# The last FFN step taken whole and put one place earlier, and a normalisation that also adds zero: attention and FFN in one kernel on Trainium2

## The chip, the cores and the metric

The kernel runs on one core of a Trainium2 chip. The metric is the device time of one execution in microseconds. The core's engines are named as in the profile: PE (matrix products), PEld (its weight loads), DVE (vector), ACT (activation functions and copies), POOL (GpSimd) and SP (which issues the transfers).

## The reference, cut to what matters

Attention over a window of 96 positions and 8 global keys, for 4 batches of 8 heads with 768 positions of 64 values; then an FFN over 3072 tokens of 512 values, with 2048 hidden values and a rational function between its two products.

```python
scores = 0.125 * q @ k.T - slope[h] * dist;  scores = where(keep, scores, -1e9)
p = exp(scores - max);  p = p / (sum(p) + 1e-9);  x = p @ v       # tokens x 512
h = x @ w_in                                                     # 3072 x 2048
P = a0 + a1*h + a2*h**2 + a3*h**3
Q = 1 + |b0|*|h| + |b1|*h**2
out = (P / (Q + 1e-6)) @ w_out                                   # 3072 x 512
```

## The kernel before, in words

**Tiling.** 12 chunks of 256 tokens are worked through. A chunk has 8 attention units (128 tokens, two heads) and 8 FFN steps (256 of the 2048 hidden values), so there are 96 of either, numbered on through the chunks. A large loop over t writes the code: in turn t it emits the parts of attention unit t, t-2, t-4, and those of FFN step f = t - 12. So the FFN runs twelve turns behind the attention, and the last turns hold FFN work alone.

**An attention unit** u transposes q and k on PE (tile `tk`), copies them on ACT, forms the scores `s` on PE, masks them on DVE into `pr`, takes the exponential on ACT (`st_soft`, L464), sums on DVE (`stats`), and normalises `pr` in `st_norm` (L476): two multiplications by 1/sum, of 128x256 values each (128x128 where a batch begins). The first 14 units do that on DVE, all later ones on POOL. Then `pr` is copied by a transfer (`raw`), transposed on PE (`tp`), copied (`pT`) and multiplied with v (`o`). From o come the FFN's inputs `xh` and `xl`, a high and a low part of x: ACT casts xh (L540), and DVE subtracts to get xl (L541).

**An FFN step** f has these parts:
- `st_ffn1` (L250): h, 128 x 2 x 256, one bank of PSUM; each half (y = 0, 1) takes 12 products of 256 columns (four pieces of x, three products of high and low parts each). There are two h tiles.
- `st_ew1`: ACT makes u, a and s from h (L274, L275, L276); `st_ew2`: DVE makes u from u and h (L281, L282), and `side(f)` adds a and s (L283); `st_ew3`: ACT takes Ln and Exp (L290, L291) to get 1/Q into the one tile r (written q in the rows).
- `st_ew4`: DVE corrects r and forms the quotient (L295, L296, L297), ACT casts its high part into g (L305), and `side(f)` subtracts for the low part of g (L306). side is POOL for every step but the last.
- `st_ffn2` (L326): 6 products of 512 columns for each half of the 256 tokens, summed in `acc` over the 8 steps of a chunk. With a chunk's last step, acc is copied to o (L332 for the last chunk) and sent out (L335).

A chunk's weights come as 32-bit halves of doubles: transfers bring `r` (L173), ACT or POOL scale (L180, L178), POOL and DVE join the pieces (L181, L182, L184), and later L201 and L202 split them into high and low parts. That goes on until about turn 30.

**Order.** A planner sets the order of the instructions of each engine by the priorities in the tables `PRI` and `PRI_A` and by its own estimate of when each is ready. From turn 36 on (`FIXED`) PE alone runs in the order in which the code is written.

**The last step** (f = 95). Its two halves are taken one after the other: first product of half 0, then that half's whole chain `last_half` (ew1 to ew4), then the first product of half 1, and its chain. All of it is written behind the second product of step 92, with the second products of steps 93, 94 and 95 behind it.

Of the kernel before, what the change touches and what calls it, by code (L numbers as in the profile page):

```python
# [14 lines left out]
ALU = mybir.AluOpType  # L15
# [32 lines left out]
           ffn1b=550, ew1=600, ew4=650, ew2=700, ffn2a=750, pT=800, ffn2b=850, dec=900, wsplit=990)  # L48
PRI_A = dict(PRI, ffn1a=800, pv=1650, qkE=950, x=1650, split=-700, ew3=2400, norm=1800, raw=1801, ffn1b=900, ew1=1050,
             ew4=850, ew2=2400, ffn2a=-400, pT=850, ffn2b=2050, dec=1850, wsplit=1090)  # L50
# [50 lines left out]
def tile_kernel(ctx: ExitStack, tc: tile.TileContext, q, k, v, n_global, n_local,  # L101
                w_in, w_out, ca, cb, out):
    nc = tc.nc
# [11 lines left out]
    NU = NCH * UPC  # L115
# [118 lines left out]
    def st_ffn1(f, y):  # L234
        c, j = divmod(f, FPC)
        if y == 0:
            hps[f] = pl.ps_h.tile(sh, F32, tag="h", name=f"h{f}")
        jw, fw = divmod((2 * j + y) * P, 2 * TOK)
        fs = slice(fw, fw + P)
        if c == 0 and not pl.split:  # L240
            for ct in range(NCT):
                nc.tensor.matmul(out=hps[f][:, y, :], lhsT=full[1, ct, jw][:, fs], rhs=xT[c][:, ct, :],  # L242
                                 start=(ct == 0), stop=(ct == NCT - 1))
            return
        xh, xl = xT[c]
        n = 0
        for ct in range(NCT):
            wh, wl = w_hi((1, ct, jw)), low[1, ct, jw]
            for w, x in ((wh, xh), (wh, xl), (wl, xh)):
                nc.tensor.matmul(out=hps[f][:, y, :], lhsT=w[:, fs], rhs=x[:, ct, :],  # L250
                                 start=(n == 0), stop=(n == 3 * NCT - 1))
                n += 1
# [5 lines left out]
    def is_last(f):  # L258
        return f == NU - 1 and not pl.split

    def side(f):
        return nc.vector if is_last(f) else nc.gpsimd

# [27 lines left out]
    def st_ew4(f, ys=BOTH):  # L293
        u, a, r = ew[f]["u"][:, ys], ew[f]["a"][:, ys], rps[f][:, ys]
        nc.vector.scalar_tensor_tensor(out=u, in0=u, scalar=a0, in1=r, op0=ALU.add, op1=ALU.mult)  # L295
        nc.vector.scalar_tensor_tensor(out=r, in0=a, scalar=q1, in1=r, op0=ALU.add, op1=ALU.mult)  # L296
        nc.vector.scalar_tensor_tensor(out=u, in0=r, scalar=2.0, in1=u, op0=ALU.subtract, op1=ALU.mult,  # L297
                                       reverse0=True)
        if f < FPC and not pl.split:
            gs[f] = u  # L300
            return
        if f not in gs:
            gs[f] = pl.ffn.tile([P, 2, 2, TOK], FR, tag="g", name=f"g{f}", bufs=pl.gbufs)
        g = gs[f]
        nc.scalar.copy(out=g[:, 0, ys], in_=u)  # L305
        side(f).tensor_tensor(out=g[:, 1, ys], in0=u, in1=g[:, 0, ys], op=ALU.subtract)  # L306

    def last_half(f, y):
        for st in (st_ew1, st_ew2, st_ew3, st_ew4):
            st(f, slice(y, y + 1))  # L310

    def st_ffn2(f, t):
        c, j = divmod(f, FPC)
# [157 lines left out]
    def st_norm(u):  # L471
        i = unit(u)[4]
        pr, st = prob[u]
        for x in range(2):
            d = blocks_of(pr[:, x], i)
            (nc.vector if u < NORMS else nc.gpsimd).tensor_scalar(  # L476
                out=d, in0=d, scalar1=st[:, 6 + x:7 + x], scalar2=None, op0=ALU.mult)

# [66 lines left out]
    def windowed():  # L547
        st_load(0, True)
        nc.sync.dma_start(out=ni[:, 0:2], in_=n_local.bitcast(I32).partition_broadcast(P))
        nc.sync.dma_start(out=ni[:, 2:4], in_=n_global.bitcast(I32).partition_broadcast(P))  # L550
        make_identity(nc, ident)
        for x in range(2):
            nc.gpsimd.memset(qzero[(1 - x) * D:(2 - x) * D, :, x, :], 0.0)
        nc.vector.tensor_copy(out=nf, in_=ni)
        nl, ng = nf[:, 0:1], nf[:, 2:3]
        scr = tmp("scr").rearrange("p a (b w) -> p (a b) w", w=P)
        scr = [scr[:, x, :] for x in range(4)]
        window_masks(nc, scr, mask0, masks, nl, ng)
        st_load(2, True)
        load_v(0)  # L560
        load_v(2)
        nc.vector.tensor_copy(out=ident_r, in_=ident)
        load_coef()

        base = tc.cur_priority
        for t in range(NU + LAG + F2):
            f = t - LAG
            pri = PRI_A if f < FPC else PRI
            u0 = t - 3 - run_of(t - 4)
            if t == FIXED:  # L570
                ctx.enter_context(tc.manual_schedule(engines={mybir.EngineType.PE}))

            def on(name, fn, u, *args):
                if 0 <= u < NU:
                    tc.cur_priority = base + 1000 * t + pri[name]
                    fn(u, *args)

            if t % 2 == 0:
                on("load", st_load, t + 4)
            if t > FIXED:  # L580
                on("pT", st_pT, t - 4)
            if t >= FIXED:
                on("qkT", st_qkT, t)
            on("score", st_score, t - 2)
            on("soft", st_soft, t - 2)
            on("ffn1a", st_ffn1, f, 0)
            if t < FIXED:
                on("qkT", st_qkT, t)
                if u0 % run_of(t - 4) == 0:
                    on("pv", st_pv, u0)  # L590
                    on("x", st_x, u0)
            on("qkE", st_qkE, t)
            if t:
                on("split", st_split, t + 1)
            if not is_last(f - 1):
                on("ew3", st_ew3, f - 1)
            on("norm", st_norm, t - 2)
            on("raw", st_raw, t - 2)
            if is_last(f):
                st_ew4(f - 1)  # L600
                last_half(f, 0)
                st_ffn1(f, 1)
                last_half(f, 1)
            else:
                on("ffn1b", st_ffn1, f, 1)
                on("ew1", st_ew1, f)
                if not is_last(f - 1):
                    on("ew4", st_ew4, f - 1)
                on("ew2", st_ew2, f)
            if t >= FIXED and u0 % 4 == 0:  # L610
                on("pv", st_pv, u0)
                on("x", st_x, u0)
            on("ffn2a", st_ffn2, f - F2, 0)
            if t < FIXED:
                on("pT", st_pT, t - 3)
            on("ffn2b", st_ffn2, f - F2, 1)
            for n, (kind, j) in enumerate(WSCHED.get(t, ())):
                tc.cur_priority = base + 1000 * t + pri["dec"] + 50 * n
                (load_win if kind else load_wout)(j)
            for n, key in enumerate(list(full)[SPLITS.get(f - 1, 0):SPLITS.get(f, 0)]):  # L620
                tc.cur_priority = base + 1000 * t + pri["wsplit"] + 4 * n
                split_w(key)
        tc.cur_priority = base + 1000 * (NU + LAG + F2 + 4)
# [154 lines left out]
```

## Time and profile before

| | |
|---|---|
| runs shown | 766.95, 763.85 and 766.6 us; median 766.6 us |
| profiled execution | 764.81 us, with a span of 763.0 us from its first to its last instruction |
| PE busy | 724.8 us, 95% of the span |
| DVE, ACT, POOL busy | 81%, 77%, 62% |
| mean granted PE clock | 0.983 of full speed |

The span is what the rows of the trace cover; 1.81 us of the execution's own time lie outside it. PE's matmuls are pipelined, so that one row's end overlaps the next row's start: what one of them costs is read from start to start.

### The profile page before, as it was taken

The numbers are of one execution on the slowest core, as the hardware profiler recorded it, in microseconds if no ns is written. First come the engines' busy times: TensorE is split into PE (matmuls) and PEld (weight loads), VectorE is DVE, ScalarE is ACT, GpSimd is POOL, SyncE is SP. The second block draws the span as 40 slices with busy tenths as digits, with TensorE's granted clock in tenths as the row PEclk, the third lists the DMA queues.
The fourth block names the chain that finished last, engine by engine and source line by source line (L and its number), as shares of the span: only waits on it lengthen the run. The fifth ranks groups of instructions, "written<-read, shape, count | busy, mean of one in ns | idle before, by whom it ended". The sixth has DMA issues, their size and how long they took to land.

```text
span 763.0 us, 15903 instructions
## 1 busy us (share of the span) xinstructions
PE 724.8 (95%) x4992; PEld 630.5 (83%) x4992; DVE 619.3 (81%) x1610; ACT 584.0 (77%) x1433; POOL 470.6 (62%) x502
## 2 busy tenths in 40 slices
PE   5579997999999999999999999999999999999985
PEld 4467665788999889989989889989989889988974
DVE  6989999887888888888788888888788888876663
ACT  6685867777978878877878878878888878875662
POOL 3575688979665666655656665665655765754440
PEclk9898998999999999999999999999999999999998
DMA  8665544232423433434433444434424333310000
GB/s 205 194 190 155 166 143 119 70 78 71 118 73 117 129 115 119 143 101 118 128 89 119 129 116 122 139 103 118 132 89 132 114 99 96 101 36 15 29 1 33
DMA packets 134014, 83.21 MB, mean 109 GB/s; under 512 B 85024, under 2 KB 114720, under 8 KB 133920
## 3 DMA queue, kind: packets, MB, share of 16 engines
q1 hardware_dynamic: 133920, 82.10, 36.9%
q8 instruction: 42, 0.69, 0.4%
q14 instruction: 52, 0.43, 0.2%
HBM read 35.92 MB, written 6.29 MB: 55 GB/s over the span
## 4 chain that ended last, share of the span: by engine, by line
PE 81%; DVE 7%; ACT 4%; DMA 4%; POOL 2%; issue 1%; SPq 0%; POOLq 0%; DVEq 0%; ACTq 0%
PE acc L326 32%; PE h L250 31%; PE o L518 5%; PE s L441 5%; PE tp L497 3%; DMA r<-in_moe_w_in_dram 2%; PE tk L380 2%; DVE r L182 1%; PE acc L321 1%; PE s L436 1%; PE h L242 1%; DMA r<-in_moe_w_out_dram 1%; DVE pr L454 1%; DMA raw<-pr 1%; DVE pr L476 1%
## 5 line engine op out<-in xcount | busy, mean ns | idle before, releaser
L326 PE MATMUL acc<-wout_h,g 128*128 128x512 f32 x704 | 238.5, 399 | 0.8 <-POOL g L306 0.8
L476 POOL TENSOR_SCALAR pr<-pr,stats 128x256 f32<-128x256 f32 (+1 forms) x164 | 143.7, 887 | 105.6 <-DVE stats L469 42.9
L250 PE MATMUL h<-xh,win_h 128*128 128x256 f32 x704 | 201.2, 286 | 4.8 <-DVE fu L282 4.8
L250 PE MATMUL h<-xl,win_h 128*128 128x256 f32 x704 | 199.5, 283 | 0.0
L283 POOL TENSOR_TENSOR fa<-fa,fs 128x512 f32<-128x512 f32 x95 | 125.2, 1318 | 83.3 <-ACT fs L276 80.3
L326 PEld LDWEIGHTS acc<-wout_h,g 128*128 128x128 f32 x704 | 131.6, 189 | 31.5 <-POOL g L306 2.5
L250 PEld LDWEIGHTS h<-xh,win_h 128*128 128x128 f32 x704 | 134.7, 191 | 7.1 <-DVE fu L282 5.5
L250 PEld LDWEIGHTS h<-xl,win_h 128*128 128x128 f32 x704 | 133.2, 189 | 2.1 <-issue 1.0
L306 POOL TENSOR_TENSOR g<-fu,g 128x512 fp32r<-128x512 f32 x87 | 113.4, 1303 | 22.9 <-ACT g L305 13.5
L295 DVE SCALAR_TENSOR_TENSOR fu<-fu,coef,q 128x512 f32<-128x512 f32 (+1 forms) x97 | 71.8, 740 | 40.7 <-ACT q L291 36.6
L464 ACT ACTIVATE pr<-pr,stats 128x256 f32<-128x256 f32 (+1 forms) x192 | 92.4, 483 | 14.0 <-DVE stats L454 12.8
L281 DVE TENSOR_TENSOR fu<-fu,h 128x512 f32<-128x512 f32 (+1 forms) x97 | 65.6, 676 | 39.4 <-ACT fs L276 39.3
L274 ACT ACTIVATE fu<-h,coef 128x512 f32<-128x512 f32 (+1 forms) x97 | 75.1, 774 | 25.8 <-PE h L250 21.2
L290 ACT ACTIVATE fs<-fa,coef 128x512 f32<-128x512 f32 (+1 forms) x97 | 69.6, 718 | 30.1 <-POOL fa L283 26.4
L416 ACT ACTIVATE qT<-tk 64x128 fp32r<-64x128 f32 x144 | 39.0, 271 | 50.8 <-PE s L441 42.3
L282 DVE SCALAR_TENSOR_TENSOR fu<-fu,coef,h 128x512 f32<-128x512 f32 (+1 forms) x97 | 71.4, 737 | 1.2
L296 DVE SCALAR_TENSOR_TENSOR q<-fa,coef,q 128x512 f32<-128x512 f32 (+1 forms) x97 | 72.1, 743 | 0.0
L297 DVE SCALAR_TENSOR_TENSOR fu<-q,fu 128x512 f32<-128x512 f32 (+1 forms) x97 | 66.2, 682 | 1.6
L275 ACT ACTIVATE fa<-h,coef 128x512 f32<-128x512 f32 (+1 forms) x97 | 65.5, 675 | 2.4 <-PE acc L321 2.4
L276 ACT ACTIVATE fs<-h,coef 128x512 f32<-128x512 f32 (+1 forms) x97 | 66.2, 683 | 0.0
L305 ACT CAST g<-fu 128x512 fp32r<-128x512 f32 (+1 forms) x89 | 55.3, 621 | 14.0 <-DVE fu L297 13.7
L454 DVE CUSTOM_DVE_ANT_0 pr<-s,masks 128x256 f32<-128x256 f32 x160 | 60.9, 416 | 2.0 <-PE s L436 0.8
(243 smaller groups left out, 1610.1 us busy)
## 6 DMA issues: line engine op xcount, KB each, us to landing
raw<-pr SPq DMA_DIRECT2D x58, 256.0 KB
sp<-nat SPq DMA_DIRECT2D x36, 256.0 KB
qT<-qT SPq DMA_DIRECT2D x144, 64.0 KB
r<-in_moe_w_in_dram SPq DMA_DIRECT2D x16, 512.0 KB
r<-in_moe_w_out_dram SPq DMA_DIRECT2D x16, 512.0 KB
nat<-in_q_dram SPq DMA_DIRECT2D x48, 128.0 KB
nat<-in_k_dram SPq DMA_DIRECT2D x48, 128.0 KB
vt<-in_v_dram SPq DMA_DIRECT2D x48, 128.0 KB
```

Source lines behind the costliest of these rows:

```text
L250: nc.tensor.matmul(out=hps[f][:, y, :], lhsT=w[:, fs], rhs=x[:, ct, :], start=(n == 0), stop=(n == 3 * NCT - 1))
L274: nc.scalar.activation(out=u, in_=h, func=AF.Identity, scale=a3, bias=a2)
L282: nc.vector.scalar_tensor_tensor(out=u, in0=u, scalar=a1, in1=h, op0=ALU.add, op1=ALU.mult)
L283: side(f).tensor_tensor(out=a, in0=a, in1=s, op=ALU.add)
L290: nc.scalar.activation(out=s, in_=a, func=AF.Ln, bias=q1)
L295: nc.vector.scalar_tensor_tensor(out=u, in0=u, scalar=a0, in1=r, op0=ALU.add, op1=ALU.mult)
L296: nc.vector.scalar_tensor_tensor(out=r, in0=a, scalar=q1, in1=r, op0=ALU.add, op1=ALU.mult)
L306: side(f).tensor_tensor(out=g[:, 1, ys], in0=u, in1=g[:, 0, ys], op=ALU.subtract)
L326: nc.tensor.matmul(out=acc, lhsT=gs[f][:, z, y, ts], rhs=w, start=(ft == 0 and n == 0), stop=(ft == NFT - 1 and n == 2))
L454: nc.vector.tensor_tensor_reduce(out=blocks_of(pr[:, x], i), in0=blocks_of(s_ps[:, x], i), in1=mk, scale=-(2.0 ** -(h + 1)), scalar=3e38, ...
L464: nc.scalar.activation(out=d, in_=d, func=AF.Exp, scale=-1.0, bias=st[:, x:x + 1], accum_out=st[:, 2 + 2 * x:3 + 2 * x])
L476: (nc.vector if u < NORMS else nc.gpsimd).tensor_scalar(out=d, in0=d, scalar1=st[:, 6 + x:7 + x], scalar2=None, op0=ALU.mult)
```

## The change

- P's normalisation (L476) gets a second operation, an addition of 0.0, on DVE and on POOL alike. Its result is the same.
- `last_half` goes. The last step has one chain over both halves, as every other step.
- PE's order at the end: both halves of the first product of step 95 stand right behind those of step 94, ahead of the second products of steps 92, 93 and 94.
- The addition of a and s (L283) and the subtraction for g (L306) of the last two steps, 94 and 95, are on DVE; before, those of step 95 alone.

```diff
     def side(f):
-        return nc.vector if is_last(f) else nc.gpsimd
+        return nc.vector if f >= NU - 2 and not pl.split else nc.gpsimd
...
-    def last_half(f, y):
-        for st in (st_ew1, st_ew2, st_ew3, st_ew4):
-            st(f, slice(y, y + 1))
...
             (nc.vector if u < NORMS else nc.gpsimd).tensor_scalar(
-                out=d, in0=d, scalar1=st[:, 6 + x:7 + x], scalar2=None, op0=ALU.mult)
+                out=d, in0=d, scalar1=st[:, 6 + x:7 + x], scalar2=0.0, op0=ALU.mult, op1=ALU.add)
...
-            on("ffn1a", st_ffn1, f, 0)
+            if not is_last(f):
+                on("ffn1a", st_ffn1, f, 0)
...
-            if not is_last(f - 1):
-                on("ew3", st_ew3, f - 1)
+            on("ew3", st_ew3, f - 1)
...
-            if is_last(f):
-                st_ew4(f - 1)
-                last_half(f, 0)
-                st_ffn1(f, 1)
-                last_half(f, 1)
-            else:
+            if not is_last(f):
                 on("ffn1b", st_ffn1, f, 1)
-                on("ew1", st_ew1, f)
-                if not is_last(f - 1):
-                    on("ew4", st_ew4, f - 1)
-                on("ew2", st_ew2, f)
+            if is_last(f + 1):
+                for y in range(2):
+                    on("ffn1b", st_ffn1, f + 1, y)
+            on("ew1", st_ew1, f)
+            on("ew4", st_ew4, f - 1)
+            on("ew2", st_ew2, f)
```

The rows below name an instruction by its line, operation and tiles (written<-read; a number behind a name is the step's or unit's, the one behind the underscore a buffer's). In the changed kernel the lines behind L306 stand four to seven lower, so that L541 becomes L537, L372 L368 and L332 L328.

**The end, on DVE.** Before, the work on the last step comes in halves (128x256), between the rows of step 94 (fu94, q94):

```order
L281 TENSOR_TENSOR fu95_9836<-fu95_9836,h95_9814 128x256
L283 TENSOR_TENSOR fa95_9837<-fa95_9837,fs95_9838 128x256
L297 SCALAR_TENSOR_TENSOR fu94_9787<-q94_9827,fu94_9787 128x512
L282 SCALAR_TENSOR_TENSOR fu95_9836<-fu95_9836,coef_64,h95_9814 128x256
L295 SCALAR_TENSOR_TENSOR fu95_9836<-fu95_9836,coef_64,q95_9845 128x256
L296 SCALAR_TENSOR_TENSOR q95_9845<-fa95_9837,coef_64,q95_9845 128x256
L297 SCALAR_TENSOR_TENSOR fu95_9836<-q95_9845,fu95_9836 128x256
L306 TENSOR_TENSOR g95_9851<-fu95_9836,g95_9851 128x256
L281 TENSOR_TENSOR fu95_9836<-fu95_9836,h95_9814 128x256
L283 TENSOR_TENSOR fa95_9837<-fa95_9837,fs95_9838 128x256
```

In the changed kernel, from the addition of a and s of step 94 on:

```order
L283 TENSOR_TENSOR fa94_9813<-fa94_9813,fs94_9814 128x512
L282 SCALAR_TENSOR_TENSOR fu94_9812<-fu94_9812,coef_64,h94_9759 128x512
L281 TENSOR_TENSOR fu95_9842<-fu95_9842,h95_9787 128x512
L283 TENSOR_TENSOR fa95_9843<-fa95_9843,fs95_9844 128x512
L295 SCALAR_TENSOR_TENSOR fu94_9812<-fu94_9812,coef_64,q94_9839 128x512
L296 SCALAR_TENSOR_TENSOR q94_9839<-fa94_9813,coef_64,q94_9839 128x512
L282 SCALAR_TENSOR_TENSOR fu95_9842<-fu95_9842,coef_64,h95_9787 128x512
L297 SCALAR_TENSOR_TENSOR fu94_9812<-q94_9839,fu94_9812 128x512
L306 TENSOR_TENSOR g94_9851<-fu94_9812,g94_9851 128x512
L295 SCALAR_TENSOR_TENSOR fu95_9842<-fu95_9842,coef_64,q95_9869 128x512
L296 SCALAR_TENSOR_TENSOR q95_9869<-fa95_9843,coef_64,q95_9869 128x512
L297 SCALAR_TENSOR_TENSOR fu95_9842<-q95_9869,fu95_9842 128x512
```

All rows are whole (128x512), and steps 94 and 95 alternate. L283 and L306 of step 94 are new on DVE; they came from POOL. L306 of step 95 and the copy of o follow.

**The end, on ACT.** Before, Ln of step 94 and then the halves of step 95:

```order
L290 ACTIVATE fs94_9789<-fa94_9788,coef_64 128x512
L274 ACTIVATE fu95_9836<-h95_9814,coef_64 128x256
L275 ACTIVATE fa95_9837<-h95_9814,coef_64 128x256
L291 ACTIVATE q94_9827<-fs94_9789 128x512
L276 ACTIVATE fs95_9838<-h95_9814,coef_64 128x256
L290 ACTIVATE fs95_9838<-fa95_9837,coef_64 128x256
L305 CAST g94_9833<-fu94_9787 128x512
L291 ACTIVATE q95_9845<-fs95_9838 128x256
L305 CAST g95_9851<-fu95_9836 128x256
L274 ACTIVATE fu95_9836<-h95_9814,coef_64 128x256
```

Now, from the first row of step 94 on:

```order
L274 ACTIVATE fu94_9812<-h94_9759,coef_64 128x512
L275 ACTIVATE fa94_9813<-h94_9759,coef_64 128x512
L276 ACTIVATE fs94_9814<-h94_9759,coef_64 128x512
L305 CAST g93_9821<-fu93_9732 128x512
L274 ACTIVATE fu95_9842<-h95_9787,coef_64 128x512
L275 ACTIVATE fa95_9843<-h95_9787,coef_64 128x512
L290 ACTIVATE fs94_9814<-fa94_9813,coef_64 128x512
L276 ACTIVATE fs95_9844<-h95_9787,coef_64 128x512
L291 ACTIVATE q94_9839<-fs94_9814 128x512
L290 ACTIVATE fs95_9844<-fa95_9843,coef_64 128x512
L305 CAST g94_9851<-fu94_9812 128x512
L291 ACTIVATE q95_9869<-fs95_9844 128x512
```

The three rows that read h95 stand ahead of Exp of step 94; Exp of step 95 stands behind the cast of g94.

**Turns 18 to 36, PE.** The planner's order changes here too, on all engines, though the text of the code does not. In turn 20, before (h8 is the first step of the second chunk, tk21 a transpose of q and k, tp17 and s19 attention):

```order
L250 MATMUL h8_1233<-xh1_705,w1_3_0l_1037 128x256
L497 MATMUL tp17_1283<-ident_70,pr17_1146 128x128 x4
L436 MATMUL s19_1319<-k2_203,qzero_69 128x256 x2
L372 MATMUL tk21_1343<-ident_70,nat20_909 128x128 x2
L518 MATMUL o8_1346<-pT17_1288,vt16_602 64x128 x2
```

Now:

```order
L368 MATMUL tk20_1246<-ident_70,nat20_909 128x128 x2
L250 MATMUL h8_1233<-xh1_705,win_h_59 128x256
L493 MATMUL tp17_1283<-ident_70,pr17_1146 128x128 x4
L432 MATMUL s19_1319<-k2_203,qzero_69 128x256 x2
L368 MATMUL tk21_1343<-ident_70,nat20_909 128x128 x2
L250 MATMUL h8_1233<-xl1_706,win_h_59 128x256
```

Seven of the 24 products of h8 now stand ahead of tp17, s19 and tk21, and 17 behind them; all 24 stood ahead.

**The same turns, DVE.** xl1 from o7 is an input of h8. Before:

```order
L281 TENSOR_TENSOR fu6_1088<-fu6_1088,h6_1068 128x512
L282 SCALAR_TENSOR_TENSOR fu6_1088<-fu6_1088,coef_64,h6_1068 128x512
L541 TENSOR_TENSOR xl1_706<-o7_1161,xh1_705 128x2x128
L182 SCALAR_TENSOR_TENSOR r0_13_1119<-r0_13_1119 128x512
L184 SCALAR_TENSOR_TENSOR w0_13f_1118<-w0_13f_1118,r0_13_1119 128x512
```

Now:

```order
L295 SCALAR_TENSOR_TENSOR fu6_1088<-fu6_1088,coef_64,q6_1176 128x512
L296 SCALAR_TENSOR_TENSOR q6_1176<-fa6_1089,coef_64,q6_1176 128x512
L184 SCALAR_TENSOR_TENSOR w0_15f_1132<-w0_15f_1132,r0_15_1133 128x512
L537 TENSOR_TENSOR xl1_706<-o7_1161,xh1_705 128x2x128
L281 TENSOR_TENSOR fu7_1185<-fu7_1185,h7_1153 128x512
```

xl1 from o7 stood ahead of the decoding of weights r0_13 to r0_15 (L182, L184); now it stands behind that of all three. On POOL the rows L181 of r0_13 and four of the splits L202 move ahead of one or two normalisations, and from turn 36 to the end the orders of DVE, ACT, POOL and SP differ in places by a row or two.

## Prediction

> **What bounds the kernel now.** I read the busy shares first, then the chain of waits, then the busy time by stretches of time.
>
> ```profile
> PE 724.8 (95%) x4992; PEld 630.5 (83%) x4992; DVE 619.3 (81%) x1610; ACT 584.0 (77%) x1433; POOL 470.6 (62%) x502
> PE 81%; DVE 7%; ACT 4%; DMA 4%; POOL 2%; issue 1%; SPq 0%; POOLq 0%; DVEq 0%; ACTq 0%
> ```
>
> PE is busy for 95% of the span, and 81% of the chain that ended last is PE's. In the stretches (columns: length, then each engine's busy time with its instructions, the granted PE clock, the transfers) the rest sits at the start and in two more places:
>
> ```profile
> 0.00:95.00 95.00, 74.11 (x354) 54.22 (x355) 81.57 (x238) 66.54 (x185) 54.08 (x67) 0.93 0.64 182
> 95.00:114.00 19.00, 17.77 (x86) 12.00 (x85) 19.00 (x38) 13.03 (x34) 15.50 (x16) 1.00 0.47 138
> 114.00:133.00 19.00, 15.13 (x81) 9.72 (x80) 17.27 (x29) 15.29 (x36) 16.44 (x18) 0.83 0.45 129
> 133.00:735.00 602.00, 601.16 (x4395) 540.65 (x4394) 489.55 (x1285) 478.96 (x1160) 380.63 (x401) 1.00 0.34 100
> 735.00:763.00 28.00, 16.62 (x82) 13.95 (x80) 11.89 (x23) 10.21 (x21) 3.92 (x4) 0.91 0.07 23
> ```
>
> From 133 us to 735 PE hardly idles: the row leaves it 0.8 us of 602. There a faster DVE, ACT or POOL has almost nothing to give. PE idles 20.9 us up to 95, where weights and the first units come in, in an order that the change keeps to turn 18, 1.23 us from 95 to 114 and 3.87 us from 114 to 133, where all engines are loaded, and at the end. The chain of waits at the end, in order of time (start, length, what):
>
> ```profile
> 733.27 2.83 PE h L250 x24
> 738.90 1.48 PE h L250 x12
> 744.53 0.40 DVE fu L282
> 744.97 2.93 PE h L250 x12
> 747.90 8.34 PE acc L326 x36
> ```
>
> The first half of h95 takes 1.48 us for 12 products. The second half starts at 744.97, when the first half's chain has left the bank: 4.59 us of idle PE. It then takes 2.93 us, because the clock has dropped:
>
> ```profile
> 744.00:745.00 1.00, 0.03 (x1) 0.03 (x1) 0.92 (x2) 0.94 (x2) 0.00 (x0) 0.70 0.00 0
> 745.00:746.00 1.00, 1.00 (x5) 1.00 (x6) 0.49 (x2) 0.47 (x2) 0.69 (x1) 0.50 0.00 0
> 748.00:749.00 1.00, 1.00 (x6) 0.83 (x5) 0.00 (x0) 1.00 (x3) 0.00 (x0) 1.00 0.00 0
> ```
>
> So the way of taking the last step costs 4.59 + 1.45 = 6.0 us of PE. Without it, PE would end near 750.2, if g95 were ready. It won't be; that sets the gain.
>
> **The change part by part: the end.** Durations of the rows I use (start, duration, engine):
>
> ```profile
> 736.13 0.78 ACT L274 ACTIVATE fu<-h,coef 128x512 f32<-128x512 f32 x1 [0.91 <-PE h L250]
> 736.82 0.68 ACT L275 ACTIVATE fa<-h,coef 128x512 f32<-128x512 f32 x1
> 737.38 0.69 ACT L276 ACTIVATE fs<-h,coef 128x512 f32<-128x512 f32 x1
> 737.96 0.62 ACT L305 CAST g<-fu 128x512 fp32r<-128x512 f32 x1
> 738.10 0.69 DVE L281 TENSOR_TENSOR fu<-fu,h 128x512 f32<-128x512 f32 x1 [0.71 <-ACT fs L276]
> 738.83 0.75 DVE L282 SCALAR_TENSOR_TENSOR fu<-fu,coef,h 128x512 f32<-128x512 f32 x1
> 739.41 1.28 POOL L306 TENSOR_TENSOR g<-fu,g 128x512 fp32r<-128x512 f32 x1
> 739.48 0.73 ACT L290 ACTIVATE fs<-fa,coef 128x512 f32<-128x512 f32 x1 [0.90 <-POOL fa L283]
> 741.22 0.60 ACT L291 ACTIVATE q<-fs 128x512 f32<-128x512 f32 x1
> 741.86 0.75 DVE L295 SCALAR_TENSOR_TENSOR fu<-fu,coef,q 128x512 f32<-128x512 f32 x1 [2.29 <-ACT q L291]
> 742.52 0.75 DVE L296 SCALAR_TENSOR_TENSOR q<-fa,coef,q 128x512 f32<-128x512 f32 x1
> 743.85 0.68 DVE L297 SCALAR_TENSOR_TENSOR fu<-q,fu 128x512 f32<-128x512 f32 x1
> ```
>
> From start to start an instruction that need not wait costs some 0.08 less than its duration on either engine (L295 to L296: 0.66; L274 to L275: 0.69). L281 starts when L276 ends, in this row; I keep that.
>
> I walk the new order from 736.10, where h94 ends (L274 reads it at 736.13), and leave all before it unmoved.
>
> 1. PE: h95 whole, 736.10 + 24 x 1.48/12 = 739.06 at most; at h94's pace of 2.83, 738.93. Its bank was read last by L282 of step 93, at 734. Then acc for 92 and 93, 2.8 each (36 products in 8.34): to 744.5. g93's subtraction is no longer behind L283 of step 94 on POOL and ends near 740, in time.
> 2. ACT: L274 and L275 of 95 at 738.96 and 739.65; Ln of 94 at 740.2; L276 of 95 at 740.9 to 741.55; Exp of 94 to 742.05. DVE: L281, L283, L282 of 94 from 738.10 to 740.1. L281 of 95 waits for L276: 741.6; L283 of 95 742.2; L295 of 94 742.8, L296 743.45, L282 of 95 744.1, L297 of 94 744.8 to 745.5.
> 3. ACT casts g94, 745.5 to 746.1. Exp of 95 is queued behind that cast: to 746.65. DVE subtracts for g94 (as L297, 0.69): to 746.85. Then L295, L296, L297 of 95: 746.8 to 748.9; cast to 749.55; subtraction to 750.3.
> 4. PE: acc of 94 can begin at 746.15, after 1.6 us of idling. Its third product needs the low part, 746.9, and ten more take 2.3: 749.2. acc of 95 begins at 749.6; its third product at 750.3; end 752.65. The copy of o and the way out stay as they are.
>
> PE ended at 756.24, so the end gains 3.6 us. The second products of steps 92 and 93 cover 5.6 us of the chain's wait, where before they covered none of it; what is late next is g94, then g95. If the clock fell in the gap of 1.6 us, up to 1.45 us would go (the row of 2.93 against 1.48). Above it fell between 744 and 745, over 3.6 us after PE fell idle, so I count nothing.
>
> One cost is left: L283 of 94 is now on DVE while POOL subtracts for g93, both with two inputs in SBUF. This pair of engines shows what that can cost:
>
> ```profile
> 126.09 0.68 DVE L184 SCALAR_TENSOR_TENSOR w_14f<-w_14f,r 128x512 int32<-128x512 int32 x1
> 126.69 1.75 DVE L184 SCALAR_TENSOR_TENSOR w_15f<-w_15f,r 128x512 int32<-128x512 int32 x1
> 126.09 1.80 POOL L283 TENSOR_TENSOR fa<-fa,fs 128x512 f32<-128x512 f32 x1
> ```
>
> Of two like instructions, the one that met POOL's L283 took 1.75 instead of 0.68. Here Ln of 94 has 0.8 us of slack behind L283, so that at most 0.3 to 0.5 us of a 1.07 us stall reaches the end. I take 0.2. Ends of this term: -4.2 and -1.5; taken: -3.4.
>
> The Trainium skill (SBUF — State Buffer, Who interferes with whom) speaks against moving L283: a DVE instruction with two SBUF inputs contends with a GpSimd instruction that reads SBUF. The rows of 1.75 and 1.80 agree. By that rule as an exclusive lock the whole 0.5 is paid, and the end gains 3.1 instead of 3.4.
>
> **The normalisation.** Rows of POOL by shape, with count, busy time and mean; and the range over all calls of two lines (min/median/max):
>
> ```profile
> L476 POOL TENSOR_SCALAR pr<-pr,stats 128x256 f32<-128x256 f32 x140 | 129.4, 935 | 95.1 <-DVE stats L469 42.2 <-ACT q L291 35.2 <-ACT fa L275 14.7
> L476 POOL TENSOR_SCALAR pr<-pr,stats 128x128 f32<-128x128 f32 x24 | 14.3, 609 | 10.5 <-ACT q L291 6.7 <-DMA raw<-pr 3.1 <-DVE stats L469 0.7
> L178 POOL TENSOR_SCALAR w_0f<-r 128x512 f32<-128x512 f32 x2 | 3.0, 1524 | 1.0 <-DMA r<-in_moe_w_in_dram 0.7 <-DVE stats L454 0.2
> L181 POOL TENSOR_SCALAR r<-r x32: 647/728/1510, 13.3 to 121.7; 128x512 int32<-128x512 uint16 x32
> ```
>
> L476 has one operation: 0.61 us for 128 columns and 0.93 for 256, so 2.5 ns a column and 0.28 fixed. L178, also one, fits: 1.52 for 512. L181 has two (multiply, add) and takes 0.65 for 512: 0.7 ns a column over the same 0.28. A second operation has thus no price here, and the nearest rows say that multiply-and-add runs three times faster than one multiplication. L181 reads 16-bit values and has constants for both operands, so it is near, not the same. Ends: 0.47 us (L181's pace) and 1.59 (twice L178's pace per column); I take 0.47 to 0.55, as L181 is the only row with two operations. POOL then loses some 65 us of its 470.
>
> What is it worth? From 133 us on at most those 0.8 us, most of them waits on other work: -0.2. On DVE the 28 early ones could gain or lose 0.1 each: nothing I can place, so 0.
>
> The Trainium skill (GPSIMD Engine Reference, 3.1 Elementwise) says that a body of up to two operations an element is bound by its ports at about one cycle, so that one and two cost alike. The rows of 1.52 and 0.65 differ from that. By it L476 would stay at 0.93, and the third rival below would hold.
>
> **The planner's new order, turns 18 to 36.** This edit costs most to price. The place before:
>
> ```profile
> 116.52 5.00 DMA r<-in_moe_w_out_dram
> 121.68 0.73 POOL L181 TENSOR_SCALAR r<-r 128x512 int32<-128x512 uint16 x1 [0.34 <-DMA r<-in_moe_w_out_dram]
> 122.49 2.37 DVE L182 SCALAR_TENSOR_TENSOR r<-r 128x512 int32<-128x512 int32 x2
> 119.75 0.42 DVE L541 TENSOR_TENSOR xl<-o,xh 128x256 fp32r<-128x256 f32 x1 [1.34 <-ACT xh L540]
> 126.74 0.69 PE L372 MATMUL tk<-ident,nat 128*128 128x128 f32 x2 [2.36 <-ACT k L402]
> 111.90 1.12 PE L321 MATMUL acc<-w_10f,fu 128*128 128x512 f32 x2 [1.04 <-DVE w_10f L184]
> ```
>
> xl1 from o7 (L541) was ready at 120.2, and h8 ran through. Now it stands on DVE behind the decoding of r0_15, whose transfer lands at 121.5 and whose L181 ends at 122.4. Behind it come L182 (0.7), the masks of unit 18 (0.75), a cast (0.5), L295 and L296 (1.3), L184 (0.7): xl1 near 126.9, some 6.7 us later. 17 products of h8 (2.0 us warm) then start behind it, and end near 129; o8, which stood at 128.5 before (tk21 waits 2.36 until 126.74, then PE waits again for pT), follows. Against that, w0_10 is decoded a place earlier, which takes most of the 1.04 us that PE waited at 111.90. Ends: -4 (both waits go, and the slow clock with them) and +4 (xl1 meets two stalls of 1.07 on DVE, and h8 runs at half clock, +2). I take +1.0: 0.5 to 1 later at o8, part of h8 slow, part of the 1.04 won. Behind 133 us PE is full, so this goes to the end as it is.
>
> On SP the transfers change places by a row or two, from turn 24 on; PE shows no wait for them after 133 us, so 0, with up to +0.5.
>
> **Sum.** -3.4 - 0.2 + 1.0 = -2.6 us on the execution of 764.81: 762.2. The median of the runs shown, 766.6, is 1.8 above that execution; in its terms I forecast 764.0, 0.3% faster. About 0.5% (3.8 us) is what a measurement can tell from no change.
>
> **The rivals.**
> - The planner's order gains. The PE waits at 111.90 (1.04) and ahead of tk21 (2.36) go, since POOL is done 0.4 us earlier with each normalisation and Ln follows it sooner. Then -3.4 - 0.2 - 2.6 = -6.2: 760.4. For it: ACT and DVE wait for POOL there. Against: xl1's new place, and r0_15, which no engine hastens.
> - Slower: xl1 comes still later. It decides if h8's rest starts past 131 us, 4 us behind my 126.9, with the clock at half: +7 there, net +3.4: 770.0. For it: POOL's splits collide with DVE there, and two or three stalls of 1.07 each would be needed. Against: ACT would still give PE its transposes.
> - The addition doesn't speed POOL up: L476 stays at 0.93 or grows. The end gains as computed, but the planner's order, if it reckons with a faster POOL, has L283 and the splits late: -3.4 + 2 = -1.4: 765.2.
> - The end gains less, as g94 or the clock is worse: -1.5 - 0.2 + 1.0: 765.9.
>
> **How the numbers follow.** Forecast 0.45; order gains 0.27; slower 0.08; no faster POOL 0.10; end gains less 0.10. Faster by over 0.5% (under 762.8): most of the order's case and a sixth of the forecast's, 0.33. Slower by over 0.5%: 0.05. The rest, 0.62, is within. The range leaves out the slower case and the far side of the order's gain: 759.8 to 767.8.
>
> **What would show it.** The end right: h95 as one run of 24 products right behind h94, PE's last row 3 to 4 us nearer to h94's end than the 20.1 us before, PE idle near 1.6 us ahead of acc of 94, clock 1.00. The norm right: L476 on POOL at 0.47 to 0.55. The order right: PE waits for xl1 (DVE L537) between 121 and 127 us. Wrong would be: PE idle above 1 us anywhere from 140 to 735, or a clock of 0.5 in the last 15 us.

## The result, and the profile after

| | before | after |
|---|---|---|
| median of 13 runs each | 766.95 us | 762.28 us |
| lowest and highest run | 763.85, 768.90 | 759.86, 765.46 |
| profiled execution (its span) | 764.81 (763.0) | 763.7 (761.9) |

The ratio is 0.9943, with a 95% interval of 0.9929 to 0.9957: 4.4 us faster, 3.3 to 5.4 us (the medians differ by 4.7). The forecast was 764.0 in a range of 759.8 to 767.8. The two profiled executions differ by only 1.1 us, since that of before lies 2.1 below its median and that of after 1.4 above its own. So the traces are compared part by part here, and the total is left to the medians.

PE's load, the stretches and the chain at the end of the changed kernel, as they were shown of before:

```profile
PE 728.0 (96%) x4992; PEld 633.4 (83%) x4992; DVE 621.1 (82%) x1605; ACT 580.6 (76%) x1427; POOL 397.8 (52%) x500
```

```profile
95.00:114.00 19.00, 18.19 (x86) 12.21 (x86) 19.00 (x37) 14.49 (x34) 12.86 (x15) 1.00 0.57 169
114.00:133.00 19.00, 13.33 (x53) 8.19 (x53) 16.02 (x31) 13.16 (x32) 16.70 (x18) 0.78 0.31 94
133.00:735.00 602.00, 602.00 (x4409) 542.37 (x4409) 491.58 (x1287) 477.93 (x1165) 315.92 (x402) 1.00 0.35 101
735.00:763.00 28.00, 18.65 (x100) 14.62 (x98) 13.40 (x20) 10.28 (x17) 4.39 (x3) 0.94 0.07 23
```

```profile
735.73 5.67 PE h L250 x48
741.48 0.41 ACT fu L274
742.16 0.68 ACT fa L275
742.84 0.61 ACT fs L290
747.32 0.61 DVE fu L297
747.96 0.63 ACT g L305
752.91 2.62 PE acc L322 x10
```

The row from 114 us shows PE worse off than before (13.33 against 15.13); from 133 us to 735 it now never idles (602.00). At the end the 4.59 us of idle PE and the half at slow clock are gone: h94 and h95 are one run of 48 products. What is left is a wait for g94 and a short one for g95 (timeline of PE; the bracket is the idle time ahead and what ended it):

```profile
748.63 0.50 PE L322 MATMUL acc<-wout_h,g 128*128 128x512 f32 x1 [1.64 <-ACT g L305]
752.11 0.50 PE L322 MATMUL acc<-wout_h,g 128*128 128x512 f32 x1 [0.15 <-ACT g L305]
```

And the normalisation on POOL, by shape, with its mean in ns:

```profile
L472 POOL TENSOR_SCALAR pr<-pr,stats 128x256 f32<-128x256 f32 x140 | 68.7, 504 | 93.4 <-DVE stats L465 64.8 <-ACT fa L275 10.9 <-DMA nat<-in_k_dram 9.8
```

It takes 504 ns instead of 935.

For the profiled executions I took three lengths from the timeline of PE: the start of h4 (the row `h<-x,w_2f` near 78 us, ahead of every row that the change moves), from there to the first product of h94, and from that to the end of PE's last row. The first row of before, and then all of after:

```profile
78.09 0.59 PE L242 MATMUL h<-x,w_2f 128*128 128x256 f32 x2
```

```profile
79.17 0.59 PE L242 MATMUL h<-x,w_2f 128*128 128x256 f32 x2
735.56 0.28 PE L250 MATMUL h<-xh,win_h 128*128 128x256 f32 x1
755.13 0.39 PE L322 MATMUL acc<-wout_h,g 128*128 128x512 f32 x1
```

So after: 79.17, then 735.56 - 79.17 = 656.39, then 755.13 + 0.39 - 735.56 = 19.96. The kernels named e1 to e11 are those of the next section. The last column is 45 us less PE's busy time in that stretch. One of the six executions of e10 took 1005.46 us at a mean granted clock of 0.658, and its ratio is that of the other five.

| kernel | start of h4 | to h94 | h94 to the end | PE idle, 95 to 140 us |
|---|---|---|---|---|
| before | 78.09 | 655.02 | 23.12 | 5.1 |
| after | 79.17 | 656.39 | 19.96 | 6.5 |
| e1 | 80.01 | 655.00 | 23.40 | 8.2 |
| e2 | 77.72 | 654.44 | 20.73 | 5.0 |
| e3 | 79.81 | 653.67 | 19.73 | 6.0 |
| e4 | 77.14 | 654.13 | 19.03 | 6.3 |
| e5 | 78.89 | 654.36 | 19.04 | 6.8 |
| e8 | 75.74 | 655.74 | 19.83 | 6.3 |
| e11 | 77.52 | 654.20 | 19.93 | 5.9 |

The first column scatters over 4.3 us among kernels whose rows up to there stand in the same order: one profile tells the start to no better than that. The clock that PE was granted up to 75 us goes with it in part: it was 0.93 in e8, which starts h4 first, and 0.86, 0.86 and 0.84 in the three that start it last (after, e3, e1), but 0.91 in e5, which is hardly earlier, and 0.86 in e2. The third column repeats to 0.3 us wherever the end is the same (before and e1; after and e11; e4 and e5), with one exception (e2, below). The kernels left out of the table have another order or pace on the way; their third column is 19.05 (e6), 19.91 (e7), 20.72 (e9) and 17.94 (e10).

### The profile page after: what moved, and what is told of

It is laid out like the page before. It is cut to its first block, busy times and chain, and to the rows that moved or that the text cites. A ratio compares the mean times of both kernels' runs of the same rounds, so it can differ in the third digit from the quotient of the medians.

```text
span 761.9 us, 15909 instructions
## 1 busy us (share of the span) xinstructions
PE 728.0 (96%) x4992; PEld 633.4 (83%) x4992; DVE 621.1 (82%) x1605; ACT 580.6 (76%) x1427; POOL 397.8 (52%) x500
## 4 chain that ended last, share of the span: by engine, by line
PE 83%; DVE 8%; issue 2%; POOL 2%; ACT 1%; DMA 1%; SPq 1%; ACTq 0%; DVEq 0%; POOLq 0%
PE h L250 33%; PE acc L322 32%; PE o L514 5%; PE s L437 5%; PE tp L493 4%; PE s L432 2%; DVE r L182 2%; PE tk L376 2%; PE acc L317 1%; DMA r<-in_moe_w_in_dram 1%; DVE pr L472 1%; DVE fu L295 1%; POOL r L181 1%; DVE pr L450 1%; DVE q L296 1%
## 5 line engine op out<-in xcount | busy, mean ns | idle before, releaser
L283 POOL TENSOR_TENSOR fa<-fa,fs 128x512 f32<-128x512 f32 x94 | 122.3, 1301 | 147.2 <-ACT fs L276 133.3
L472 POOL TENSOR_SCALAR pr<-pr,stats 128x256 f32<-128x256 f32 (+1 forms) x164 | 77.4, 485 | 114.4 <-DVE stats L465 70.3
L306 POOL TENSOR_TENSOR g<-fu,g 128x512 fp32r<-128x512 f32 x86 | 112.7, 1310 | 19.6 <-DVE qT L417 12.9
L281 DVE TENSOR_TENSOR fu<-fu,h 128x512 f32<-128x512 f32 x96 | 65.7, 684 | 45.1 <-ACT fs L276 45.0
L290 ACT ACTIVATE fs<-fa,coef 128x512 f32<-128x512 f32 x96 | 69.6, 725 | 35.4 <-POOL fa L283 33.4
L274 ACT ACTIVATE fu<-h,coef 128x512 f32<-128x512 f32 x96 | 74.7, 778 | 28.6 <-PE h L250 24.3
L295 DVE SCALAR_TENSOR_TENSOR fu<-fu,coef,q 128x512 f32<-128x512 f32 x96 | 71.5, 745 | 26.5 <-ACT q L291 24.1
L282 DVE SCALAR_TENSOR_TENSOR fu<-fu,coef,h 128x512 f32<-128x512 f32 x96 | 71.2, 741 | 1.0
L296 DVE SCALAR_TENSOR_TENSOR q<-fa,coef,q 128x512 f32<-128x512 f32 x96 | 71.8, 748 | 0.0
L297 DVE SCALAR_TENSOR_TENSOR fu<-q,fu 128x512 f32<-128x512 f32 x96 | 66.1, 688 | 1.2
L275 ACT ACTIVATE fa<-h,coef 128x512 f32<-128x512 f32 x96 | 65.2, 679 | 2.2 <-PE acc L317 2.2
L276 ACT ACTIVATE fs<-h,coef 128x512 f32<-128x512 f32 x96 | 66.0, 687 | 0.0
```

Of the source, the lines that this page charges most:

```text
L274: nc.scalar.activation(out=u, in_=h, func=AF.Identity, scale=a3, bias=a2)
L282: nc.vector.scalar_tensor_tensor(out=u, in0=u, scalar=a1, in1=h, op0=ALU.add, op1=ALU.mult)
L283: side(f).tensor_tensor(out=a, in0=a, in1=s, op=ALU.add)
L290: nc.scalar.activation(out=s, in_=a, func=AF.Ln, bias=q1)
L472: (nc.vector if u < NORMS else nc.gpsimd).tensor_scalar(out=d, in0=d, scalar1=st[:, 6 + x:7 + x], scalar2=0.0, op0=ALU.mult, op1=ALU.add)
```

## The experiments

Ratios are to the kernel before, run beside them on the same chip.

**e1, the zero alone.**

```diff
 the kernel before, and in st_norm:
-  scalar2=None, op0=ALU.mult)
+  scalar2=0.0, op0=ALU.mult, op1=ALU.add)
```

> The kernel before with the zero added in the normalisation and nothing else; its instruction order up to the last steps is that of the changed kernel. Theory A (the end gave 3.0 us of the 4.4, the zero the other 1.4 by a quicker start): 1.4 us faster than before, ratio 0.998, PE idle of 4 to 5 us ahead of the second half of h95 as before. Theory B (the end gave all, the two starts differ by chance): within 0.5 us, ratio 1.000. Theory C (the zero gave most): 3 us or more, ratio 0.996 or less. Under all of them POOL's normalisation of 128x256 takes 0.50 us instead of 0.93.

Measured: 0.9992 (0.9974 to 1.0011), 765.97 against 766.42 us. L476 on POOL is at 0.48 us (median of both shapes). Theory C falls; A and B both lie in the interval.

**e2, the end alone.**

```diff
 the changed kernel, and in st_norm:
-  scalar2=0.0, op0=ALU.mult, op1=ALU.add)
+  scalar2=None, op0=ALU.mult)
```

> The changed kernel with one multiplication in the normalisation, as before; up to the last steps its instructions stand as in the kernel before. Theory A: 3.0 us faster than before, ratio 0.996; from the start of h94 to PE's last row 20.0 us, as in the changed kernel (23.0 before). Theory B: 4.4 us, ratio 0.994. Theory C: 1.5 us or less, ratio 0.998. If the zero's faster POOL helped at the end too, the 20.0 us would be longer here.

Measured: 0.9966 (0.9946 to 0.9986), 2.6 us. The zero and the end add up: 0.6 + 2.6 = 3.2 us. A's 0.996 fits and B's 0.994 lies just outside; C's 0.998 is inside, but e1 showed that the zero is not the larger part. The end was 20.73 us long, 0.77 more than after, with the same idle time of 1.64 ahead of g94. The stretches around it (length, busy times, then PE's clock) show why:

```profile
743.00:744.00 1.00, 0.58 (x3) 0.14 (x1) 1.00 (x3) 0.00 (x0) 0.00 (x0) 1.00 0.00 0
744.00:745.00 1.00, 0.00 (x0) 0.00 (x0) 0.52 (x1) 0.45 (x1) 0.00 (x0) 1.00 0.00 0
746.00:747.00 1.00, 1.00 (x4) 0.83 (x5) 1.00 (x2) 0.00 (x0) 0.00 (x0) 0.85 0.00 0
747.00:748.00 1.00, 1.00 (x3) 0.78 (x3) 0.91 (x2) 0.00 (x0) 0.00 (x0) 0.50 0.00 0
```

PE stopped near 743.6. The clock fell to half at about 746.7 (0.85 is the mean of that microsecond), 3.1 us later and after PE was back at work, and stayed there to 750. In the six profiles with this idle time (after, e2, e7, e8, e9, e11) it fell in two: in e9 at about 771.5 us, 3.0 us after PE had stopped, and there too the end is some 0.8 us longer (20.72). And with the zero missing, three waits of PE are back, 0.8 us in sum. They stand in the waits of PE from 140 to 730 us, as in the kernel before, whose row is:

```profile
PE acc L326 <- POOL g L306: 0.8, 3, 0.3
```

In the changed kernel that list is empty.

**e3, h95 whole, but in its own turn.**

```diff
 the changed kernel, and in the loop:
-            if not is_last(f):
-                on("ffn1a", st_ffn1, f, 0)
+            on("ffn1a", st_ffn1, f, 0)
 ...
-            if not is_last(f):
-                on("ffn1b", st_ffn1, f, 1)
-            if is_last(f + 1):
-                for y in range(2):
-                    on("ffn1b", st_ffn1, f + 1, y)
+            on("ffn1b", st_ffn1, f, 1)
```

> The changed kernel with the first product of step 95 whole, but in its own turn, behind the second product of step 92. Theory A (h95 ahead of step 92 puts L274 and L275 of step 95 ahead of Ln of 94 on ACT, and this costs step 94 more than the earlier h95 wins): 0.6 us faster than the changed kernel, ratio to before 0.993 to 0.994; from h94's start to PE's last row 19.4 us. Rival (the early place of h95 is what makes the end short): 1.5 to 2.8 us slower than the changed kernel, 21.5 to 22.8 us, since h95 starts 2.8 us later.

Measured: 0.9942 (0.9922 to 0.9963); the end 19.73 us. The rival falls: the early place of h95 wins nothing. The end is shorter than the changed kernel's, as A says, but by 0.2 us and not 0.6: PE waits 0.69 for the low part of g94 and 1.08 for g95. What gained at the end was to take step 95 whole, not to take it early.

**e4, the last rows of ACT and DVE in written order.**

```diff
 the changed kernel, in the turn of step 95:
+            by_hand.enter_context(tc.manual_schedule(engines={PE, Activation, DVE}))
 st_ew3(94); st_ew1(95)
-            on("ew4", st_ew4, f - 1)
-            on("ew2", st_ew2, f)
+            st_ew4(f - 1, last=lambda: st_add(f))   # L283 of 95 ahead of L306 of 94
+            st_mul(f)                               # L281, L282 of 95
```

> The changed kernel with the last rows of ACT and DVE in an order written out: step 94's Ln and Exp ahead of step 95's L274, and 94's L295 to L297 ahead of 95's L281; all else in the same order. Theory A (the 1.64 us that PE waits for g94 come from that order): the wait ahead of the second product of 94 goes, PE's last row stands 18.3 us behind h94's start instead of 20.0, ratio to before about 0.992. Rival (the length of step 95's own chain sets the end whatever the order): 19.7 to 20.3 us, no difference to the changed kernel.

Measured: 0.9931 (0.9909 to 0.9953); the end 19.03 us, so that the rival falls. The wait for g94 went, as A says, but 0.7 of the 1.7 expected did not come: now PE waits 1.45 for g95, since DVE has no gap left. Exp of 95 (ACT L298) was done at 743.17; L302 of 95 started at 744.04, behind L289 and L290 of 95, which had been behind L315 of 94:

```profile
746.94 0.50 PE L331 MATMUL acc<-wout_h,g 128*128 128x512 f32 x1 [1.45 <-ACT g L312]
742.57 0.60 ACT L298 ACTIVATE q<-fs 128x512 f32<-128x512 f32 x1
743.19 0.75 DVE L290 SCALAR_TENSOR_TENSOR fu<-fu,coef,h 128x512 f32<-128x512 f32 x1
744.04 0.75 DVE L302 SCALAR_TENSOR_TENSOR fu<-fu,coef,q 128x512 f32<-128x512 f32 x1
```

**e5, the zero from unit 40 on, end as e4.**

```diff
 e4, and in st_norm:
+            if u >= 40: ... scalar2=0.0, op0=ALU.mult, op1=ALU.add
+            else:       ... scalar2=None, op0=ALU.mult
```

> The changed kernel with the last rows of ACT and DVE by hand, and the zero added only from unit 40 on: the early instructions stand as in the kernel before, POOL's normalisation is short from about 170 us on. Theory A (in the steady part the zero is worth 0.84 us, three waits of PE of 0.28 for POOL's g, and the new early order costs 1 to 2 us of PE): no wait of PE over 0.15 us from 140 us to the end part; PE idles 5.0 us from 95 to 140 us (6 to 8 with the zero everywhere); 1 us faster than with the zero everywhere, ratio to before 0.991 to 0.992. Theory B (the early order is worth nothing either way; starts differ by chance): same as with the zero everywhere, 0.993. Theory C (the early order gains): 0.994 or more.

Measured: 0.9918 (0.9888 to 0.9947), which tells A from B as little as from C. In its trace PE idled 6.8 us from 95 to 140, not 5.0, with the instructions as before; and one of the three waits of 0.28 stayed, at 263 us. Inconclusive on the early order.

**e7, the zero up to unit 39 alone.**

```diff
 the changed kernel, and in st_norm:
+            if u < 40: ... scalar2=0.0, op0=ALU.mult, op1=ALU.add
+            else:      ... scalar2=None, op0=ALU.mult
```

> The changed kernel with the zero added only up to unit 39. Theory A: PE's three waits of 0.28 us for POOL's g, near 260, 430 and 600 us, are back, since POOL's normalisation takes 0.93 us there; from 95 to 140 us PE idles as in the changed kernel, 6 to 8 us. Rival (those waits went with the new order, not with the short normalisation): they stay away.

One run: 776.64 us, 10 us slower than before, which neither theory had. Waits of PE from 140 to 730 us (sum, count, longest):

```profile
PE acc L322 <- ACT g L305: 4.0, 2, 2.0
PE acc L322 <- POOL g L306: 3.8, 4, 2.3
```

The rows of PE and of POOL there:

```profile
325.01 0.50 PE L322 MATMUL acc<-wout_h,g 128*128 128x512 f32 x1 [2.03 <-ACT g L305]
328.09 1.22 PE L322 MATMUL acc<-wout_h,g 128*128 128x512 f32 x2 [2.34 <-POOL g L306]
324.98 1.82 POOL L476 TENSOR_SCALAR pr<-pr,stats 128x256 f32<-128x256 f32 x2 [5.31 <-ACT g L305]
326.77 1.27 POOL L306 TENSOR_TENSOR g<-fu,g 128x512 fp32r<-128x512 f32 x1
```

PE's rows stand as in the changed kernel; those of DVE, ACT and POOL don't. At 323 us the cast of g is late, and on POOL two normalisations, 0.91 each, stand ahead of the subtraction for the same g, so that PE waits 2.03 and then 2.34 us; at 361 us it waits 2.01 and 0.87 in the same way. Two of the three 0.28s came back (447, 618 us), as A says. So at 0.93 us a normalisation, POOL's place in the steady part hangs on how the planner's order falls.

**e9, a maximum as the second operation.**

```diff
-  scalar2=0.0, op0=ALU.mult, op1=ALU.add)
+  scalar2=0.0, op0=ALU.mult, op1=ALU.max)
```

> The changed kernel with a maximum with 0.0 as the second operation in place of the addition (the values are positive, so nothing changes); the order of the instructions follows its own plan. Theory A (it is the pair of multiply and add that POOL runs quickly): L472 on POOL takes 0.93 us or more for 128x256, as with one multiplication. Rival (any second operation makes it quick): 0.50 us.

```profile
L472 POOL TENSOR_SCALAR pr<-pr,stats 128x256 f32<-128x256 f32 x140 | 160.4, 1157 | 65.4 <-DVE stats L465 49.5 <-ACT q L291 7.4 <-ACT fs L290 5.9
```

```profile
PE acc L322 <- POOL g L306: 7.5, 13, 2.0
PE acc L322 <- ACT g L305: 4.0, 2, 2.0
```

One run: 786.97 us. The instruction takes 1157 ns, more than the 935 of one multiplication: the rival falls. Not a second operation as such makes L472 short, but this pair. With 1.16 us a call PE waits 11.5 us for g between 140 and 730 us (the two rows of waits), with 0.93 it waits 0.8 us in the kernel before and 7.8 in e7, and with 0.50 in the changed kernel not at all. The planner's order differs in each, so this is the worth of the pace and of the order made for it.

**e8, only the last step's L283 and L306 on DVE.**

```diff
-        return nc.vector if f >= NU - 2 and not pl.split else nc.gpsimd
+        return nc.vector if is_last(f) else nc.gpsimd
```

> The changed kernel with L283 and L306 of step 94 on POOL, as before; those of 95 alone on DVE. Theory A (POOL would take 1.30 instead of 0.69 for each, but starts L283 of 94 at once, and DVE wins two places): Ln of 94 no later than 0.1 us, the low part of g94 0.6 later; from h94's start to PE's last row 19.6 to 20.6 us against 20.0. Rival (moving them to DVE was what made the end short): 21.2 us or more.

One run: 759.46 us; the end 19.83 us against 19.96. PE waits 0.67 us for the low part of g94, which now comes from POOL, but no longer for g95. Moving step 94's two instructions to DVE is worth nothing in this profile, as A says.

**e11, the zero on POOL alone.** The edit: DVE's normalisations have one multiplication.

> The changed kernel with the zero on POOL alone; the 28 normalisations on DVE have one multiplication, as before. The order of the instructions is that of the changed kernel. Theory A (on DVE the zero is worth nothing): ratio to before 0.994 to 0.995, as the changed kernel; L472 on DVE at 0.35 us, like with the zero. Rival (the later start of the kernels with the zero, 77 to 80 us against 78 at the first whole h, comes from a slower DVE): 1 us faster than the changed kernel, 0.993, and the 20 DVE rows of 128x256 shorter than with the zero.

Measured: 0.9946 (0.9925 to 0.9967). On DVE the 128x256 form takes 467 ns in the mean here and 517 in the changed kernel, but 435 and 468 in e3 and e4, which have the zero too: the zero isn't seen on DVE. The start of h4 at 77.52 lies within the scatter. The rival falls.

**e6, the zero in the scaling of the weights too, end as e4.**

```diff
 e4, and at L178:
-  scalar1=2.0 ** -112, scalar2=None, op0=ALU.mult)
+  scalar1=2.0 ** -112, scalar2=0.0, op0=ALU.mult, op1=ALU.add)
```

> The changed kernel with the last rows by hand, and with a zero added also in the scaling of the weights on POOL (L178, 12 calls of 1.5 to 2.1 us, 128x512). Theory A (multiply-and-add runs on POOL at the pace of L181, 0.7 ns a column): L178 takes 0.65 to 0.75 us, POOL wins 11 to 14 us ahead of 95 us; PE's idle time up to 60 us, 19.2 to 19.8 us, gets shorter by 0 to 2 us, the rest of it set by transfers and DVE; ratio to before 0.991 to 0.993. Rival (in that part transfers and DVE set everything, and a new order there costs): L178 short all the same, ratio 0.993 to 0.996.

Measured: 0.9886 (0.9861 to 0.9910), 757.65 us: the gain is more than either said. Theory A's pace holds in six of the ten calls of L178 (the expectation counted twelve), 0.66 to 0.75 us; the other four take 0.82 to 1.17. All ten take 8.1 us against 16.8 in e4, so POOL wins 8.7 us there and not 11 to 14. Rows of L178 (min, median, max in ns), then the stretch up to 133 us, of e4 and of e6:

```profile
L178 POOL TENSOR_SCALAR w_1f<-r x3: 711/751/822, 33.4 to 49.8; 128x512 f32<-128x512 f32 x3
L178 POOL TENSOR_SCALAR w_0f<-r x2: 659/662/664, 14.7 to 22.0; 128x512 f32<-128x512 f32 x2
```

```profile
0.00:133.00 133.00, 107.26 (x518) 77.04 (x519) 117.88 (x308) 94.87 (x252) 82.60 (x100) 0.92 0.57 165
```

```profile
0.00:133.00 133.00, 108.46 (x550) 77.45 (x551) 118.36 (x313) 95.44 (x253) 75.81 (x102) 0.97 0.58 166
```

PE's busy time is nearly alike (107.26, 108.46); what changed is PE's clock, 0.92 to 0.97 in the mean over this stretch. It is not this profile alone: over their whole spans the four executions of e6 were granted 0.988 to 0.993, the ten of e4 0.976 to 0.985. The weights come sooner (DVE joins the pieces of w0_9 at 84.76 us instead of 89.51), PE's pauses fall elsewhere, and less of its work runs at half clock. That the L178s, and not the new order that the planner made with them, did it isn't told apart here.

**e10, the better end.** L306 of step 94 goes to POOL, and in the last second product the two products with g's low part come last in each half of the tokens.

```diff
 e6, and in st_ffn2:
+                if is_last(f) and z: continue          # low part of g: behind the others
 ...
+        if is_last(f): the two products with gs[f][:, 1, y, ts]
 in st_ew4:
-        side(f).tensor_tensor(out=g[:, 1, ys], ...)
+        (nc.vector if is_last(f) else nc.gpsimd).tensor_tensor(out=g[:, 1, ys], ...)
```

> The zero in L472 and in L178, the last rows of ACT and DVE by hand, L306 of step 94 on POOL, and in the second product of step 95 the products with the low part of g last. Theory A (after the order by hand DVE's rows of 94 and 95 set the end): 95's L295 starts when Exp of 95 ends, 0.8 us earlier, and eight products run ahead of the low part of g95 instead of two: from h94's start to PE's last row 17.7 to 18.1 us instead of 19.0; ratio to before 0.986 to 0.988. Rival (POOL's L306 meets DVE in SBUF and both take longer, as the 1.75 and 1.80 of the trace before): 18.8 to 19.5 us.

Measured: 0.9838 (0.9816 to 0.9860), 12.4 us faster than before and the best version; the median of those five executions is 754.34 us against 767.20. The end is 17.94 us long, as A says, though the edit puts four products ahead of the low part of g95 and not eight: DVE's subtraction was done when the fifth came. L303 of 95 starts at 740.73, 12.0 us behind h94's start at 728.74; in e4 L302 did so 12.8 us behind it. POOL's subtraction for g94 met no delay:

```profile
739.44 1.31 POOL L316 TENSOR_TENSOR g<-fu,g 128x512 fp32r<-128x512 f32 x1 [3.25 <-DVE fa L285]
740.73 0.75 DVE L303 SCALAR_TENSOR_TENSOR fu<-fu,coef,q 128x512 f32<-128x512 f32 x1
743.63 0.50 PE L334 MATMUL acc<-wout_h,g 128*128 128x512 f32 x1 [0.23 <-ACT g L313]
```

## Why the prediction was right, and where its sizes were off

The time came out in the range and the sign was right, but the change gained 4.4 us where I forecast 2.6; to a gain of over 0.5% I had given a chance of 0.33.

**The end** (taken -3.4, ends -4.2 and -1.5). From where L274 reads h94 to PE's end it was 20.11 us and is 755.52 - 738.59 = 16.93: -3.18. The walk held row by row: h95 right behind h94, 1.64 us of PE waiting for g94 (1.6 said), the low part of g95 next. Most of its error was in the last ten products, 2.3 us said and 2.62 measured, the row at 752.91. (One remark of the walk is wrong without changing its sum: the second product of step 92 covered 2.6 us of the chain of step 94 before too, from 736.1 to 738.7.) The 0.2 for L283 of 94 was not paid on DVE but on POOL:

```profile
741.16 0.68 DVE L283 TENSOR_TENSOR fa<-fa,fs 128x512 f32<-128x512 f32 x1
741.17 1.84 POOL L306 TENSOR_TENSOR g<-fu,g 128x512 fp32r<-128x512 f32 x1 [3.62 <-issue]
```

DVE, first by 0.01, ran at its usual 0.68; POOL's took 1.84 instead of 1.30, and g93 had that time. The Trainium skill (SBUF — State Buffer, Who interferes with whom) says that the order of issue decides which of the two blocks; the trace agrees, with 0.54 on the one that came second.

I counted nothing for the clock in a gap of 1.6 us, and in the changed kernel's profile it held; e2 and e9 show that it need not: +0.77 in e2. How often it falls in the changed kernel no run tells. The Trainium skill (TensorE: Matmul & The Clock Gate, Part 1) has the clock fall after at least one idle window of about 3.4 us. In e2 it fell with 1.64 us of idling, 3.1 us after PE had stopped; the measurement decides.

**The normalisation.** The duration was right: 0.504 against 0.47 to 0.55, taken from L181, the one row with multiply and add. (The upper end of 1.59 is twice L476's own pace a column; twice L178's would be 1.52.) The Trainium skill (GPSIMD Engine Reference, 3.1 Elementwise) has a body of up to two operations bound by its ports at about one cycle an element, by which one and two would cost alike. That does not hold for this instruction: 935, 504 and 1157 ns for one multiplication, multiply and add, multiply and maximum. Its worth was mis-sized: -0.2, on the ground that most of the 0.8 us from 133 us on waited on other work. The list of PE's waits gives POOL's g as the cause of all of it, and all of it went (before, e2: 0.8; after: 0). I had read the idle time but not what ended it.

**The planner's new order** (+1.0, ends -4 and +4). It made xl1 late as I said, and more: xl1 came not at 126.9 but at 131.22, and h8's rest started at 132.21 at half clock. I had POOL end its last L181 at 122.4; it ended at 125.6, behind L283, and one L182 on DVE took 1.76.

```profile
131.22 0.41 DVE L537 TENSOR_TENSOR xl<-o,xh 128x256 fp32r<-128x256 f32 x1
132.21 0.56 PE L250 MATMUL h<-xl,win_h 128*128 128x256 f32 x1
119.23 0.90 PE L493 MATMUL tp<-ident,pr 128*128 128x128 f32 x4 [2.01 <-POOL pr L472]
128.65 1.09 PE L493 MATMUL tp<-ident,pr 128*128 128x128 f32 x4 [1.48 <-DVE stats L450]
```

Less the 1.08 us by which this profile starts h4 later, that is 131.1, just past the 131 us from which I had the slower rival decide, with +7. The +7 did not come. PE had other rows to do meanwhile; its waits were for POOL's L472 (2.01, at 119) and DVE's masks (1.48, at 128.65), not for xl1, so that the sign that I had named for the order, a wait of PE for xl1, did not show. Before, too, the clock had been at half, from 126.6 to 133.4; now it was so from 127.9 to 134.8, no longer than before. So the step that failed there is the rival's price, which took a late xl1 for an idle PE. My own +1.0 was built on the same late xl1: that its size is not contradicted is luck. From h4 to h94 the six kernels with the new order and the zero throughout take 654.9 us in the mean (653.7 to 656.4), before and e2 654.7. With 0.8 us gained in the steady part, the order costs about 1 us, with as much uncertainty as size; the idle time from 95 to 140 us, 6.5 in the mean of the six against 5.1 and 5.0, points the same way.

**The sum.** The traces account for -3.2 - 0.8 + 1 = -3.0 us; e1 and e2 give 3.2; the runs of the whole change 4.4 (3.3 to 5.4), and those of e11 4.1 (2.5 to 5.7). The 1.2 to 1.4 us between stay open, and need not be there at all: the intervals of e1 and e2 are 1.4 and 1.5 us wide to each side, and no profile tells the start better than 4 us.

**The rivals.** A normalisation not made faster fell with 0.504. What it would have cost hangs on the order: in e2, with 0.93 and the old order, nothing but the 0.8 us of waits; in e7 and e9, with 0.93 and 1.16 in orders made for them, far more than the 2 us that I allowed. The gain of the order fell: the waits at 111.90 (1.04) and ahead of tk21 (2.36) did go, but others came, 2.01 and 1.48 us ahead of tp, 0.99 for w0_11 and 0.85 ahead of a transpose.

## What to carry to other kernels

Ask of an idle engine not only how long it idles, but what ended each wait: in the steady part three waits of 0.28 us are all that the traces show for the 66 us of normalisation taken off POOL (143.7 to 77.4, both shapes), and the list of waits had named them. A last step that is cut in halves to shorten its chain can cost more than it saves, when its second half has to wait for the first one's chain; take it whole, and then look at which step's rows the planner puts first. On POOL, look for one-operation multiplications that can be written as multiply-and-add, first where weights are prepared and PE still waits.

## What the runs showed of the hardware that I had not expected

- POOL, 128x256 float32: one multiplication by a value for each partition 935 ns, multiply and add 504, multiply and maximum 1157; 128x512 with a constant, where least disturbed, 1.52 and 0.66 us.
- PE's clock fell to half 3.1 and 3.0 us after the start of a pause of 1.64 us (e2, e9), and did not in four other profiles with the same pause.
- POOL, busy for 62% of the span before, set PE's time all the same where its instruction got 0.22 us longer and the planner's order followed: 787.0 us against 767.2 (e9).
